# Buffers of their own for q, k and v, and a searched order, in a retention layer with an MLP behind it

## The chip, the cores and the metric

The kernel runs on one core of one Trainium2 chip. The metric is the device time of one execution in microseconds (us), over several runs. The engines are TensorE (PE; its weight loads are listed apart as PEld), VectorE (DVE), ScalarE (ACT), GpSimd (POOL) and SyncE (SP). POOL issues the loads, SP issues the transposing DMAs and the stores.

## The reference

For 8 batches and 8 heads, 576 positions and a head size of 64, retention without softmax: scores times a decay that is zero above the diagonal, times v. Its output is the input of an MLP with an exact Gelu.

```python
scores = scale * np.matmul(q, k.transpose(0, 1, 3, 2))
Dmat = np.where(rel >= 0, gamma[:, None, None] ** rel[None, :, :], 0.0)
attn_out = np.matmul(scores * Dmat[None, :, :, :], v)
x = attn_out.transpose(0, 2, 1, 3).reshape(B * S, H * D)     # 4608 x 512
h = x @ w_in                                                 # 512 -> 2048
g = 0.5 * h * (1.0 + erf(h * inv_sqrt2))
out = g @ w_out                                              # 2048 -> 512
```

## The kernel before

**Units.** The sequence is cut into chunks of 128 positions and a tail of 64. A *unit* is one chunk of one batch, or the tails of a pair of batches: 36 units in all. For each, q and k are turned (head dimension to the partitions), scores are made, masked with the decay, and multiplied with v; a running state (`u_ps`, `u_sb`) carries the earlier chunks. The tile `vh` is v times a decay by head. It is one multiplication on VectorE or, for the units in `VH_ACT` (L174), eight ACTIVATEs, one for each head, on ScalarE (`scaled_v`, L814). Units 0 to 9 are turned by TensorE, the later ones by transposing DMAs that SP issues (`turn_dma`, L603).

**The MLP.** Four units make a block of 512 tokens (`xT`), nine blocks in all. The first layer (`hT`) of blocks 2 to 8 is laid out by `LAYOUTS` (L192): a digit is a *unit of seven products* for a quarter of the hidden features (Strassen's scheme: 28 matmuls of 256 columns, tiles `yT`, `zT`, `xT_`, with sums made by VectorE from `xs` and `wi_sum` and folding on VectorE and ScalarE), and "p" with a digit is a plain quarter (16 matmuls of 512 columns). Two digits in one string are woven together. The second layer (`oT`) uses seven products too, from block 1 on. ScalarE does the Gelus and most copies out of PSUM.

**Loads.** q, k, v and the weights are loaded by POOL in the order of `ORDER` (L196), converted to bf16 on the way; wi and wo are eight blocks of each weight matrix. Units of a pair share a slot. A slot holds q and k in one tile and v in another, from a pool with `N_LD` = 4 buffers (`tiles_of`, L475). A buffer is handed out in turn, and the load waits for the last reader of what was in it.

**The plan.** The kernel's Python code is a list scheduler (`class Plan`, L30): each operation has an engine, an estimated duration, operations it depends on and a due time; the loop at the end takes the operation that can start first. It fixes the order of the instructions on every engine. `Ring` (L263) is what the plan knows of a buffer pool: `take` counts buffers handed out, `give` notes when one comes free, and `at` says when the next may be taken. In before, `at` sorts the times at which buffers come free and takes the n-th. `read` (L494) gives a slot back when q, k and v of both its units have had their last reader. TensorE's choice is in `pe_candidates` (L1543): MLP pieces in their order, and attention stretches (`macros`) when they are due, at least `GAP_A` or `GAP_B` after the stretch before; the groups in `APART` have their scores in a stretch of their own, `BEFORE` us ahead. Up to 16 us, gaps of TensorE are filled with warm-up matmuls (`warm`, L1515).

Of the kernel before, what the change touches and what calls it, by code (L numbers as in the profile page):

```python
# [29 lines left out]
class Plan:  # L30
# [4 lines left out]
    def __init__(self):  # L35
        self.ops = {}
        self.T = dict.fromkeys(self.ENGINES, 0.0)
        self.open = {e: [] for e in self.ENGINES}

# [42 lines left out]

    def start(self, op, engine):
        t = max(self.T[engine], op.ready)
        return max(t, op.at()) if op.at else t
# [13 lines left out]
    def run(self, op, engine, start):  # L99
        op.ran = engine  # L100
        self.T[engine] = self.T["now"] = start + self.dur(op, engine)
        if op.fn:
            op.fn(engine) if op.engine == "any" else op.fn()
        self.done(op, self.T[engine])
# [3 lines left out]
def kernel(  # L108
# [52 lines left out]
    def slot_of(i):  # L161
# [7 lines left out]
    N_LD = 4  # L169
# [4 lines left out]
    VH_ACT = [5, 8, 12, 14, 15, 17, 19, 20, 26, 28, 30, 31, 32, 35, 37]  # L174
# [10 lines left out]
    GAP_A = 4.2  # L185
    GAP_B = 1.5
    APART = [3, 6, 7]
    BEFORE = 0.4
    UNIT_FROM = 2
    LOOK = 16  # L190
    HOLD = 4.6
    LAYOUTS = {2: ['0', '12', 'p3'], 3: ['01', '2', 'p3'], 4: ['2', '30', 'p1'], 5: ['01', '2', 'p3'], 6: ['10', '2', 'p3'], 7: ['01', '23'], 8: ['3', '20', 'p1']}  # L192
    LEAD = 8
    SPREAD = 7.1
    EASE = 6.5
    ORDER = ("q3 q2 k3 q1 pos v2 k2 wi0 k1 wi4 v3 v1 wi1 wi3 wi5 v4 wi2 wi6 k4 wi7 q4 wo0 q5 k5 v5 wo4 wo1 q9 q8 "  # L196
             "wo5 v7 wo6 k7 wo7 v10 wo2 q6 v6 k6 wo3 q7 k10 q10 k8 k9 v9 v8").split()
# [8 lines left out]
    ld_pool = ctx.enter_context(tc.tile_pool(name="ld", bufs=N_LD))  # L206
# [56 lines left out]
    class Ring:  # L263
        def __init__(self, size):
            self.size, self.taken, self.free = size, 0, []

        def at(self):
            n = self.taken - self.size
            return 0.0 if n < 0 else (sorted(w.end + 0.12 if isinstance(w, Landing) else w for w in self.free)[n] if n < len(self.free) else NEVER)

        def take(self):
            self.taken += 1

        def give(self, when):
            self.free.append(when)

    ld_ring, tr_ring, vh_ring, ret_ring, x_ring = Ring(N_LD), Ring(N_QKT), Ring(N_VH), Ring(N_RET), Ring(3)
# [194 lines left out]
    loaded, slots, w_in_sb, w_out_sb = {}, {}, {}, {}  # L472
    touched = {}

    def tiles_of(i):  # L475

        if i not in loaded:
            n = slot_of(i)
            if i in kept:
                loaded[i] = (const.tile([128, 2, H, D], BF16, name=f"qk_ld{i}"), const.tile([128, H, D], BF16, name=f"v_ld{i}"))  # L480
                return loaded[i]
            if n not in slots:
                ld_ring.take()
                slots[n] = (ld_pool.tile([128, 2, H, 2, D], BF16, tag="qk", name="qk_ld"),
                            ld_pool.tile([128, 2, H, D], BF16, tag="v", name="v_ld"))
            qk, v_ld = slots[n]
            j = units[i][2] or 0
            if i in old:
                loaded[i] = (qk.rearrange("p a (j h) b d -> p j a (h b) d", j=2)[:, j], v_ld[:, j])
            else:  # L490
                loaded[i] = (qk[:, :, :, j], v_ld[:, j])
        return loaded[i]

    def read(i, what):  # L494

        n = slot_of(i)
        got = touched.setdefault(n, set())
        got.add((i, what))
        want = {(m, x) for m in pair_with(i) for x in
                ["v"] + (["turn0", "turn1"] if i < N_PE_TR else ["turn"]) + (["state"] if units[i][1] < NCI - 1 else []) + (["inner"] if i in raw else [])}  # L500
        if i not in kept and want <= got:
            ld_ring.give(turning[i] if what == "turn" else T["now"] + 0.12)

    def load_unit(what, i):
        bp, ci, j = units[i]
        qk, v_ld = tiles_of(i)
        src = {"q": q, "k": k, "v": v}[what]
        if j is None:
            both = slots[i][0]
            for jj in range(2):  # L510
                rows = slice(TAIL * jj, TAIL * jj + TAIL)
                dst = v_ld[rows] if what == "v" else both[0:TAIL, "qk".index(what), :, jj]
                nc.gpsimd.dma_start(dst, src[2 * bp + jj, :, ci * C:S, :].rearrange("h s d -> s h d"))
                move(0.68, 0.48)
            return 0.0
        dst = v_ld if what == "v" else qk[:, "qk".index(what)]
        nc.gpsimd.dma_start(dst, src[2 * bp + j, :, ci * C:ci * C + C, :].rearrange("h s d -> s h d"))  # L517
        return move(0.87, LOAD)
# [19 lines left out]
    for item in ORDER:  # L538
        what = item.rstrip("0123456789")
        i = int(item[len(what):] or 0)  # L540
        if what == "pos":
            add("pos", "pool", 0.25, prev, make_pos)
        elif what in ("wi", "wo"):
            add(item, "pool", 0.73, prev, lambda what=what, i=i: load_w(what, i), at=room_to_fly, lag=0.0)
        else:
            def fits(i=i):
                return max(room_to_fly(), 0.0 if i in kept or slot_of(i) in slots else ld_ring.at())
            add(item, "pool", 1.36 if units[i][2] is None else 0.87, prev,
                lambda what=what, i=i: load_unit(what, i), at=fits, lag=0.0)
        prev = [item]  # L550
# [21 lines left out]
    def qkT_of(i):  # L572
        n = slot_of(i)
        if n not in turned_of:
            tr_ring.take()
            turned_of[n] = tr_pool.tile([128, 2, H, TAIL if i in tails else 128], BF16, tag="qkT", name="qkT")
        if i in old:
            return turned_of[n].rearrange("p a (j hp) s -> p j a hp s", j=2)[:, i - n]
        return turned_of[n]
# [3 lines left out]
    def part_of(i, jj):  # L583

        if i in old:
            return loaded[i][0][:, jj], qkT_of(i)[:, jj]
        n = i - slot_of(i)
        return (slots[slot_of(i)][0][:, jj, 4 * n:4 * n + 4].rearrange("p h b d -> p (h b) d"), qkT_of(i)[:, jj, 4 * n:4 * n + 4])
# [14 lines left out]
    def turn_dma(i):  # L603
# [3 lines left out]
        for jj in what:  # L607
            nc.sync.dma_start(qkT_of(i)[:, jj], slots[n][0][rows, jj].rearrange("p h b d -> p (h b d)"), transpose=True)
# [46 lines left out]
    def inner(i):  # L655
        bp, ci, j = units[i]
        s = st[i]
        vals = loaded[i][1] if i in raw else s["vh"]
# [16 lines left out]
    def state(bp, ci):  # L675
# [3 lines left out]
        for h in range(H):  # L679
            for j, i in enumerate(pair_of[bp, ci]):  # L680
                product(u_ps[half(j), h, :], lhsT=loaded[i][0][:, 1, h, :], rhs=st[i]["vh"][:, h, :],
                                 start=(ci == 0 and h == 0), stop=(h == H - 1), skip_group_check=True)
        for i in pair_of[bp, ci]:
            vh_ring.give(T["pe"] + 0.3)
            read(i, "state")
# [44 lines left out]
    def state_atoms(bp, ci, t):  # L730
        return [(N64, [(u_bank[1][half(b), h, :], loaded[i][0][half(t), 1, h, :], st[i]["vh"][half(t), h, :],
# [59 lines left out]
    def gone(nm):  # L791
# [3 lines left out]
        if kind in ("in_b", "in_t"):  # L795
            ret_ring.give(T["pe"] + 0.3)
            tr_ring.give(T["pe"] + 0.3)
            if kind == "in_t":
                vh_ring.give(T["pe"] + 0.3)
        elif kind == "st_b":  # L800
            for i in pair_of[key]:
                vh_ring.give(T["pe"] + 0.3)
# [11 lines left out]
    def scaled_v(i, engine, heads=(0, H)):  # L814
        ci = units[i][1]
        if "vh" not in st[i]:
            vh_ring.take()
            st[i]["vh"] = vh_pool.tile([128, H, D], BF16, tag="vh", name="vh")
        vh = st[i]["vh"]
        if engine == "dve":  # L820
            nc.vector.tensor_tensor(vh, loaded[i][1], dv[:, :, ci:ci + 1].to_broadcast([128, H, D]), op=ALU.mult)  # L821
        else:
            for h in range(*heads):
                nc.scalar.activation(vh[:, h], loaded[i][1][:, h], AF.Copy, scale=dv[:, h, ci:ci + 1])  # L824
# [11 lines left out]
    def evacuate(i, engine):  # L836
# [8 lines left out]
        else:  # L845
            dst = x[:, :, i % 4 * C:i % 4 * C + C]
            b, o = st[slot_of(i)]["o"][j] if i in fine else st[i]["o"]
            if i not in fine:
                out_of_T.add(i)
                if out_of_T >= set(pair_with(i)):  # L850
                    tr_ring.give(T["pe"] + 0.3)
# [15 lines left out]
    tiles_of(0)  # L867
    for nm in "qkv":
        add(f"{nm}0", "any", {"act": 0.6, "dve": 0.83}, [],
            lambda engine, nm=nm: copy_on(engine, loaded[0][1] if nm == "v" else loaded[0][0][:, "qk".index(nm)], first[nm]),  # L870
# [57 lines left out]
    for i in v_order:  # L928
# [4 lines left out]
        if i in VH_ACT:  # L933
# [55 lines left out]
    def g_sum(t, two, which):  # L989
# [9 lines left out]
        nc.vector.tensor_tensor(out_, x0, x1, op=op)  # L999
# [46 lines left out]
    def x_sum(t, which):  # L1046
# [7 lines left out]
        nc.vector.tensor_tensor(xs_tiles[t][:, which], x0, x1, op=op)  # L1054
# [129 lines left out]
    def third(key, width, engine):  # L1184
        m_ring.take()
# [11 lines left out]
    def raw12(key, width, engine):  # L1197
        f_ring.take()
# [4 lines left out]
    def dif(key):  # L1203
        nc.vector.tensor_tensor(chain[key]["q"], chain[key]["X"][1], target(key, "c12") if key[0] == "2" else chain[key]["c12"],
                                op=ALU.subtract)
        if key[0] == "u":
            f_ring.give(T["dve"] + 0.12)
# [10 lines left out]
    def c11(key):  # L1218
# [3 lines left out]
        m_ring.give(T["dve"] + 0.12)  # L1222
# [3 lines left out]
    def first_of(key, width, r):  # L1226
        if "p1" not in chain[key]:
            m_ring.take()
# [7 lines left out]
    def onto(key):  # L1236
        x = chain[key]["B"][1]
        nc.vector.tensor_tensor(x, x, chain[key]["p1"], op=ALU.add)
        m_ring.give(T["dve"] + 0.12)
# [137 lines left out]
    for t in range(FAST, N_BLK):  # L1377
        for two in range(2):
            kps = [2 * two, 2 * two + 1]
            gl = gelus_of(t, kps, 0) + gelus_of(t, kps, 1)  # L1380
            for which in range(4):
                add(f"gs{t},{two}.{which}", "dve", 0.6, gl + ([f"gs{t},{two}.{which - 1}"] if which else []),
                    lambda t=t, two=two, which=which: g_sum(t, two, which),
                    begins["p", t, "5673"[which]] - 1.5 + 0.6 * two,
# [7 lines left out]
    for t in range(N_BLK):  # L1392
        if with_units[t]:
            soon = min(W["u", t, kp, "3"] for kp in with_units[t])
            for which in range(5):
                add(f"xs{t}.{which}", "dve", 0.335, [f"x{i}" for i in range(4 * t, 4 * t + 4)] + ([f"xs{t}.0"] if which else []),
                    lambda t=t, which=which: x_sum(t, which), soon - 3.0 + 0.1 * which, at=xs_ring.at if not which else None)
# [261 lines left out]
```

## Time and profile before

| what | us |
|---|---|
| median of 3 runs | 283.02 (282.54 to 283.83) |
| the profiled execution | 282.72 |
| its span in the profile | 280.7 |
| busy: TensorE, VectorE, ScalarE, POOL | 273.9, 230.1, 174.0, 110.4 |

The span goes from the first to the last instruction of the profiled execution; 2.0 us of its time lie around it. In the page's lists, a group's line is `line engine op out<-in xcount | busy us, mean ns of one | idle before, and what ended it`. A line of the waits is `engine line <- what it waited for: us in total, times, longest us`.

### The profile page before, as it was taken

Reading aid. Unit: us, or ns where it says so; the run is one execution under the profiler, and the core shown is the slowest. Engines: PE = TensorE matmul, PEld = TensorE weight load, DVE = VectorE, ACT = ScalarE, POOL = GpSimd, SP = SyncE. Lnnn points to the kernel's source line nnn. Section 1 sums busy time; section 2 is a strip of 40 time slices with the busy share of each in tenths; the row PEclk is TensorE's granted clock in tenths of the full one; section 3 lists DMA queues with packets and bytes.
Section 4 is the critical chain, followed back from the end, with each engine's and each line's share of the span. In section 5 each row is a group of like instructions: output and inputs, shape, how many; then the busy total and the mean of one; then the engine's idle time right before and its main releaser. Section 6 shows DMA issues by size and latency. Waiting matters only on the chain.

```text
span 280.7 us, 8896 instructions
## 1 busy us (share of the span) xinstructions
PE 273.9 (98%) x3731; PEld 220.0 (78%) x3731; DVE 230.1 (82%) x438; ACT 174.0 (62%) x414; POOL 110.4 (39%) x139
## 2 busy tenths in 40 slices
PE   7999999999999999999999999999999999999993
PEld 2679767578888688868887888688868888888782
DVE  5870465699999998999799999987987799969832
ACT  7678733646438952995297319852898379528740
POOL 8967778847546086233326804705000000000000
PEclk9999999999999999999999999999999999999999
DMA  9999999999999999999989999999800040022013
GB/s 148 165 182 186 178 186 165 142 238 133 127 139 173 197 114 128 140 230 145 156 188 57 134 112 172 210 117 135 184 22 2 6 149 2 4 75 77 0 40 112
DMA packets 152071, 35.57 MB, mean 127 GB/s; under 512 B 141024, under 2 KB 147680, under 8 KB 152032
## 3 DMA queue, kind: packets, MB, share of 16 engines
q0 software_dynamic: 115792, 17.97, 98.1%
q1 hardware_dynamic: 35200, 16.78, 34.9%
q8 instruction: 29, 0.48, 0.8%
q10 hardware_dynamic: 1040, 0.26, 0.4%
q14 instruction: 10, 0.08, 0.1%
HBM read 36.70 MB, written 9.44 MB: 164 GB/s over the span
## 4 chain that ended last, share of the span: by engine, by line
PE 87%; DVE 4%; POOL 4%; DMA 3%; issue 1%; ACT 0%; POOLq 0%; DVEq 0%
PE oT L229 39%; PE hT L229 16%; PE zT L229 10%; PE yT L229 7%; PE o_ps L229 4%; DMA w_in<-in_moe_w_in_dram 3%; PE sc L229 2%; POOL qk_ld L517 2%; PE u_ps L229 2%; DVE s L999 1%; PE qk_ps L233 1%; DVE ret L652 1%; POOL v_ld L517 1%; POOL w_in L523 1%; DVE g L999 0%
## 5 line engine op out<-in xcount | busy, mean ns | idle before, releaser
L229 PEld LDWEIGHTS <-g 128*128 128x128 bf16 x576 | 55.1, 98 | 12.5 <-issue 0.2
L229 PEld LDWEIGHTS <-w_in 128*128 128x128 bf16 x656 | 53.0, 98 | 13.3 <-DMA w_in<-in_moe_w_in_dram 0.4
L229 PE MATMUL hT<-xT,w_in 128*128 128x128 bf16 (+2 forms) x480 | 53.5, 266 | 0.3 <-DMA w_in<-in_moe_w_in_dram 0.3
L229 PEld LDWEIGHTS <-wi_sum 128*128 128x128 bf16 x440 | 42.8, 98 | 6.6
L1099 ACT ACTIVATE g<-hT 128x512 bf16<-128x512 f32 (+1 forms) x72 | 35.9, 505 | 19.5 <-PE hT L229 17.7
L229 PE MATMUL oT<-w_out,g 128*128 128x256 bf16 (+1 forms) x320 | 45.6, 294 | 0.0
L517 POOL DMA_DIRECT2D qk_ld<-in_q_dram x31 | 28.0, 905 | 35.1 <-DMA qkT<-qk_ld 22.8
L229 PEld LDWEIGHTS <-s 128*128 128x128 bf16 x384 | 36.8, 98 | 5.6 <-DVE s L999 0.5
L517 POOL DMA_DIRECT2D v_ld<-in_v_dram x31 | 28.1, 910 | 22.8 <-ACT vh L824 9.5
L229 PE MATMUL oT<-w_sum,s 128*128 128x256 bf16 x256 | 32.4, 273 | 0.2 <-ACT o_sb L1243 0.2
L824 ACT ACTIVATE vh<-v_ld,dv 128x64 bf16<-128x64 bf16 x112 | 31.2, 346 | 1.0 <-DMA v_ld<-in_v_dram 1.0
L229 PE MATMUL oT<-w_sum,g 128*128 128x256 bf16 x256 | 30.8, 273 | 0.0
L517 POOL DMA_DIRECT2D qk_ld<-in_k_dram x31 | 28.0, 903 | 5.5 <-DMA v_ld<-in_v_dram 5.2
L1243 ACT COPY o_sb<-oT 128x512 f32<-128x512 f32 (+1 forms) x27 | 14.5, 538 | 25.2 <-PE oT L229 13.3
L1212 ACT ACTIVATE g<-zT 128x512 bf16<-128x512 f32 x44 | 25.9, 614 | 0.1
L652 DVE TENSOR_TENSOR ret<-sc,msk 128x512 bf16<-128x512 f32 x36 | 23.2, 687 | 1.4 <-PE sc L229 1.4
L1247 DVE TENSOR_TENSOR o_sb<-o_sb,oT 128x512 f32<-128x512 f32 (+1 forms) x27 | 16.8, 629 | 8.8 <-PE oT L229 4.5
L570 ACT COPY q<-yT 128x512 f32<-128x512 f32 x18 | 10.3, 594 | 21.8 <-PE yT L229 21.8
L855 DVE TENSOR_TENSOR xT<-o_ps,dqT 128x512 bf16<-128x512 f32 x26 | 16.8, 686 | 3.3 <-PE o_ps L229 3.3
L821 DVE TENSOR_TENSOR vh<-v_ld,dv 128x512 bf16<-128x512 bf16 x22 | 15.0, 688 | 3.4 <-DMA v_ld<-in_v_dram 3.4
L1221 DVE TENSOR_TENSOR zT<-q,zT 128x512 f32<-128x512 f32 x22 | 15.3, 695 | 1.0 <-PE zT L229 0.6
L1191 DVE TENSOR_TENSOR q<-q,zT 128x512 f32<-128x512 f32 x22 | 14.5, 684 | 1.7 <-PE zT L229 0.8
(170 smaller groups left out, 453.6 us busy)
## 6 DMA issues: line engine op xcount, KB each, us to landing
out_dram<-o_sb SPq DMA_DIRECT2D x30, 256.0 KB, 3.9
qk_ld<-in_q_dram POOLq DMA_DIRECT2D x31, 128.0 KB, 7.6
qk_ld<-in_k_dram POOLq DMA_DIRECT2D x31, 128.0 KB, 8.5
v_ld<-in_v_dram POOLq DMA_DIRECT2D x31, 128.0 KB, 8.0
w_in<-in_moe_w_in_dram POOLq DMA_DIRECT2D x8, 256.0 KB, 8.6
w_out<-in_moe_w_out_dram POOLq DMA_DIRECT2D x8, 256.0 KB, 7.8
out_dram<-o_sb SPq DMA_DIRECT2D x12, 128.0 KB, 2.7
v_ld<-in_v_dram POOLq DMA_DIRECT2D x8, 64.0 KB, 6.4
```

Source lines behind the costliest of these rows:

```text
L229: return nc.tensor.matmul(*args, **more)
L517: nc.gpsimd.dma_start(dst, src[2 * bp + j, :, ci * C:ci * C + C, :].rearrange("h s d -> s h d"))
L652: nc.vector.tensor_tensor(r, t, by, op=ALU.mult)
L821: nc.vector.tensor_tensor(vh, loaded[i][1], dv[:, :, ci:ci + 1].to_broadcast([128, H, D]), op=ALU.mult)
L824: nc.scalar.activation(vh[:, h], loaded[i][1][:, h], AF.Copy, scale=dv[:, h, ci:ci + 1])
L855: nc.vector.tensor_tensor(dst, o, dqT[:, :, ci * C:ci * C + C], op=ALU.mult)
L1099: nc.scalar.activation(g_of(t, m0)[:, m0 % 2:m0 % 2 + n, m0 // 8, lo:hi], hT, AF.Gelu)
L1191: nc.vector.tensor_tensor(q_, q_, chain[key]["Z"][1], op=ALU.subtract)
L1212: nc.scalar.activation(target(key, what), chain[key][n][1], AF.Gelu)
L1221: nc.vector.tensor_tensor(to, chain[key]["q"], z, op=ALU.add)
L1243: nc.scalar.copy(target(key, what), chain[key][n][1])
L1247: nc.vector.tensor_tensor(to, to, chain[key][n][1], op=ALU.add)
```

## The change

The pool of load buffers becomes three: q has three buffers, k five, v four, each with a ring of its own, so that a buffer comes free with the last reader of its own tensor. `Ring` now notes who took which buffer, and `at` waits for the one that is next in turn; the vh and qkT rings are keyed in the same way. Four more units' `vh` stand on ScalarE (18 of the 36 instead of 14). Block 5 has two units of seven products and two plain quarters instead of three and one; other blocks have their parts in another order. The load order and seven of the plan's constants (`GAP_A`, `GAP_B`, `BEFORE`, `HOLD`, `LEAD`, `SPREAD`, `EASE`) are new, and group 5 is added to `APART`. Lists for work on POOL (`VH_POOL`, `XS_POOL`, `GS_POOL`) are there and empty; with them empty, the new `port` in `Plan` delays nothing.

```diff
-    N_LD = 4
+    N_LD = {"q": 3, "k": 5, "v": 4}
...
-    VH_ACT = [5, 8, 12, 14, 15, 17, 19, 20, 26, 28, 30, 31, 32, 35, 37]
+    VH_ACT = [5, 7, 9, 13, 14, 15, 17, 18, 20, 22, 23, 26, 27, 29, 31, 33, 34, 35, 37]
+    VH_POOL = []
+    XS_POOL = []
+    GS_POOL = []
...
-    GAP_A = 4.2
-    GAP_B = 1.5
-    APART = [3, 6, 7]
-    BEFORE = 0.4
+    GAP_A = 0.9
+    GAP_B = 0.5
+    APART = [3, 5, 6, 7]
+    BEFORE = 4.7
...
-    HOLD = 4.6
-    LAYOUTS = {2: ['0', '12', 'p3'], 3: ['01', '2', 'p3'], 4: ['2', '30', 'p1'], 5: ['01', '2', 'p3'], 6: ['10', '2', 'p3'], 7: ['01', '23'], 8: ['3', '20', 'p1']}
-    LEAD = 8
-    SPREAD = 7.1
-    EASE = 6.5
-    ORDER = ("q3 q2 k3 q1 pos v2 k2 wi0 k1 wi4 v3 v1 wi1 wi3 wi5 v4 wi2 wi6 k4 wi7 q4 wo0 q5 k5 v5 wo4 wo1 q9 q8 "
-             "wo5 v7 wo6 k7 wo7 v10 wo2 q6 v6 k6 wo3 q7 k10 q10 k8 k9 v9 v8").split()
+    HOLD = 5.3
+    LAYOUTS = {2: ['0', '12', 'p3'], 3: ['3', '20', 'p1'], 4: ['2', '30', 'p1'], 5: ['3', '2', 'p0', 'p1'], 6: ['2', '3', '0', 'p1'], 7: ['10', '23'], 8: ['2', '30', 'p1']}
+    LEAD = 8.8
+    SPREAD = 7.3
+    EASE = 8.9
+    ORDER = ("q3 k2 pos k1 q2 q1 k3 v2 v1 wi0 wi4 v3 wi5 wi1 wi6 wi2 v4 wi7 wi3 q5 wo0 k4 k5 q4 v5 wo4 k7 wo1 wo5 "
+             "v10 q9 wo2 q6 wo6 q8 wo7 k6 v6 v7 wo3 q7 q10 k10 k9 k8 v8 v9").split()
...
         def at(self):
-            n = self.taken - self.size
-            return 0.0 if n < 0 else (sorted(w.end + 0.12 if isinstance(w, Landing) else w for w in self.free)[n] if n < len(self.free) else NEVER)
+            n = len(self.taken) - self.size
+            w = self.free.get(self.taken[n], NEVER) if n >= 0 else 0.0
+            return w.end + 0.12 if isinstance(w, Landing) else w
...
-    ld_ring, tr_ring, vh_ring, ret_ring, x_ring = Ring(N_LD), Ring(N_QKT), Ring(N_VH), Ring(N_RET), Ring(3)
+    ld_ring = {what: Ring(N_LD[what]) for what in "qkv"}
+    tr_ring, vh_ring, ret_ring, x_ring = Ring(N_QKT), Ring(N_VH), Ring(N_RET), Ring(3)
...
-            if n not in slots:
-                ld_ring.take()
-                slots[n] = (ld_pool.tile([128, 2, H, 2, D], BF16, tag="qk", name="qk_ld"),
-                            ld_pool.tile([128, 2, H, D], BF16, tag="v", name="v_ld"))
+        if (what, n) not in slots:
+            ld_ring[what].take(n)
+            slots[what, n] = ld_pool.tile([128, 2, H, D] if what == "v" else [128, H, 2, D], BF16, tag=what, name=f"{what}_ld", bufs=N_LD[what])
...
-        want = {(m, x) for m in pair_with(i) for x in
-                ["v"] + (["turn0", "turn1"] if i < N_PE_TR else ["turn"]) + (["state"] if units[i][1] < NCI - 1 else []) + (["inner"] if i in raw else [])}
-        if i not in kept and want <= got:
-            ld_ring.give(turning[i] if what == "turn" else T["now"] + 0.12)
+            want = set()
+            for m in pair_with(i):
+                if i < N_PE_TR:
+                    want |= {(m, x) for x in ("turn0", "turn1") if kinds[x] == kind}
+                elif i in tails or kind == "qk"[m - n]:
+                    want |= {(m, "turn")} if kind != "v" else set()
+                want |= {(m, "state")} if kind == "k" and units[i][1] < NCI - 1 else set()
+                want |= {(m, x) for x in ["v"] + (["inner"] if i in raw else [])} if kind == "v" else set()
+            if want <= got:
+                ld_ring[kind].give(turning[i] if what == "turn" else T["now"] + 0.12, n)
...
-            def fits(i=i):
-                return max(room_to_fly(), 0.0 if i in kept or slot_of(i) in slots else ld_ring.at())
+            def fits(what=what, i=i):
+                return max(room_to_fly(), 0.0 if i in kept or (what, slot_of(i)) in slots else ld_ring[what].at())
```

## The prediction

> **What bounds the kernel now.** I read the page's busy times first, then TensorE's waits, then the busy times by stretch, then the timeline at the two places where TensorE does lose time.
>
> ```profile
> span 280.7 us, 8896 instructions
> PE 273.9 (98%) x3731; PEld 220.0 (78%) x3731; DVE 230.1 (82%) x438; ACT 174.0 (62%) x414; POOL 110.4 (39%) x139
> PEclk9999999999999999999999999999999999999999
> ```
>
> ```profile
> PE warm L229 <- DVE ln_scale L347: 1.2, 1, 1.2
> PE hT L229 <- DMA w_in<-in_moe_w_in_dram: 0.3, 1, 0.3
> PE oT L229 <- ACT o_sb L1243: 0.2, 1, 0.2
> ```
>
> These are all of TensorE's waits: it waits once for a load (the third weight block at 19.1 us) and never for q, k or v. Busy time of pipelined matmuls can hide gaps, so I also took the time from each matmul's start to the next one's and compared it with the median for the same pair of shapes. From the 49th hT matmul (19.64) to the last matmul the medians add up to 253.4 us, and the stream took 256.2. So 2.8 us is all that a perfect feeding of TensorE could give back there. Six places hold 1.0 of it: 72.4 (0.12), 82.8 (0.14), 160.3 (0.28), 161.0 (0.14), 192.3 (0.16), 242.4 (0.14). The rest is crumbs below 0.06.
>
> ```profile
> 62.00:90.00 28.00, 28.00 (x384) 24.08 (x383) 28.00 (x59) 15.33 (x34) 17.82 (x22) 1.00 2.09 148
> 146.00:162.00 16.00, 15.79 (x258) 12.22 (x256) 15.74 (x27) 9.46 (x21) 10.91 (x13) 1.00 1.64 95
> ```
>
> Columns: stretch, its length, then busy time (instructions) of PE, PEld, DVE, ACT, POOL. VectorE has no free time in either stretch, and four of the six places lie in them. In the second, TensorE's sequencer waited for a copy that waited for VectorE:
>
> ```profile
> 159.33 0.70 DVE L1238 TENSOR_TENSOR oT<-oT,q 128x512 f32<-128x512 f32 x1 [0.22 <-issue]
> 160.07 0.59 ACT L1243 COPY o_sb<-oT 128x512 f32<-128x512 f32 x1 [2.53 <-DVE oT L1238]
> 160.70 0.60 PE L229 MATMUL oT<-w_sum,s 128*128 128x256 bf16 x4 [0.21 <-ACT o_sb L1243]
> ```
>
> So three things can move the end: the start (up to about 19 us, where TensorE runs warm-up matmuls for want of data), the total of matmul work, and VectorE's two full stretches.
>
> **Part 1: buffers of their own for q, k and v; the plan hands them out in turn.** POOL waits long for free buffers:
>
> ```profile
> POOL qk_ld L517 <- DMA qkT<-qk_ld: 22.8, 3, 9.4
> POOL qk_ld L513 <- PE u_ps L229: 14.7, 2, 10.2
> POOL v_ld L517 <- ACT vh L824: 9.5, 1, 9.5
> ```
>
> All loads queued behind such a wait are late with it, and the transposing DMAs behind them on SP's queue, with the stores behind those. But by the order of the built program a transposed tile is first used 10 to 44 us of matmul time after its transpose is issued, 18 or more from the third pair on, and a transpose takes 8.6 us to land. This cover took in all the lateness of before (TensorE's waits name none). In the changed order the same distances are 10.5 to 40 us, again 18 or more from the third pair on. A q buffer now comes free with its transpose instead of with the last reader of q, k and v. I cost the part at 0. If the cover were gone, the first two pairs (10.5 and 12.3 us against 8.6) would show it first. 133 loads and 30 transposes stay.
>
> **Part 2: the start.** The load order moves wi0 from the seventh load to the ninth and puts k1, q1, k3, v1 ahead of it. Landings of before by the trace: the first at 7.50, then every 0.90; from the twelfth on, 0.85 for a q, k or v block and 1.33 for a weight block (19.99, 21.29; 23.53, 24.85). By the same steps the changed order lands v1 at 13.8, wi0 15.1 (before 12.81), wi4 16.5 (14.94), v3 17.3 (15.84), wi5 18.7. The third weight block of before came 1.2 later than these steps, at 19.14; with that, wi5 comes at 19.9. First-layer pieces of the first block (eight 128x128 matmuls, 11.79 / 26 = 0.453 us each):
>
> ```profile
> 18.30 0.62 PE L229 MATMUL hT<-xT,w_in 128*128 128x128 bf16 x8
> 19.18 11.79 PE L229 MATMUL hT<-xT,w_in 128*128 128x128 bf16 x208 [0.26 <-DMA w_in<-in_moe_w_in_dram]
> ```
>
> Before has done five at 19.18, starts the seventh at 19.63 and is dense from there. In the new order I place the pieces by landing and by the durations of copies (0.59) and masks (0.64): wi0 with unit 1's rows at 15.1; then another after unit 2's value product at 15.9; wi4 twice from 16.5 to 17.4; the state product and unit 3's value product (0.35 each) to 18.1; two pieces to 19.0, or 0.2 less where starts overlap; so the seventh at about 18.9. That is 0.7 earlier, and both streams have the same medians behind that piece. Bounds: 0 if wi5 comes at 19.9 or later and the next blocks with it (the two first blocks' eight pieces are used up at 19.8), 1.3 if no gap at all is left from 16.5 on. I take **-0.7**, since the landing steps are measured and the cast of q0, which now stands behind the position table on VectorE, ends at about 6.0, still before the warm-ups end at 6.3.
>
> **Part 3: matmul work.** 3731 matmuls become 3715: four fewer warm-ups, and block 5 has two fast units and two plain quarters instead of three and one. A unit is 28 matmuls of 256 columns at 109.7 ns = 3.07 us, a plain quarter 16 of 512 at 221.1 = 3.54: +0.47. The new order switches less often between attention and the MLP, though; summed over its whole order with the medians of each pair of shapes, the stream from the 49th hT matmul on is 253.4 us again. **0.0**, with +0.5 as the upper bound.
>
> **Part 4: VectorE and ScalarE.** Four units' vh move to ScalarE, and a unit's folding goes. By the mean of each form VectorE loses 2.7 us of durations in all, ScalarE gains 7.5. What matters is where, in 14 us of matmul time: 62-76 has 18.3 before and 18.2 after, 76-90 16.9 and 16.7, so the places at 72 and 83 stay. 146-160 falls from 16.5 to 15.1, and 230-244 from 16.2 to 15.7. VectorE starts an operation every 0.60 while one lasts 0.69 (the timeline at 146 to 162), so 14 us hold about 16.1 of durations: 146-160 drops below full. Removed: 0.28 + 0.14 at 160, perhaps 0.14 at 242. I take **-0.4** (0 to -1.0, all six places). What is late next is a ScalarE copy, below.
>
> The smaller gaps between attention stretches and the earlier scores of groups held apart move no work; I give their unknown new waits **+0.0**, -0.3 to +0.7.
>
> Sum: 282.72 (the profiled execution: 280.7 span and 2.0 around it) - 0.7 + 0.0 - 0.4 = 281.6. The median of the runs shown is 283.02, 0.3 above that execution, so the forecast for a median is **281.9**.
>
> **The rivals.**
>
> *The start gains nothing.* wi5 at 19.9 and the blocks behind it each come as TensorE asks for them; only part 4 is left: 283.0 - 0.4 = 282.6. For: the 1.2 us delay did occur in before at just this time. Against: each block feeds 4 x 0.453 = 1.8 us and takes 1.33 to land.
>
> *More than forecast.* 1.3 at the start and all six places: 283.0 - 2.3 = 280.7. Against: VectorE stays full from 62 to 90.
>
> *Slower: ScalarE becomes the late engine.* A vh is eight ACTIVATEs on ScalarE:
>
> ```profile
> L824 ACT ACTIVATE vh<-v_ld,dv 128x64 bf16<-128x64 bf16 x112 | 31.2, 346 | 1.0 <-DMA v_ld<-in_v_dram 1.0
> L821 DVE TENSOR_TENSOR vh<-v_ld,dv 128x512 bf16<-128x512 bf16 x22 | 15.0, 688 | 3.4 <-DMA v_ld<-in_v_dram 3.4
> ```
>
> At 32.28 in the timeline eight take 2.02, 0.5 for each part of two. The changed order puts 4 x 4 = 16 more such parts between the gelus and copies that free PSUM banks, above all at 146-160 (ScalarE 10.0 to 14.2 in 14 us) and 216-230 (9.0 to 14.0). If a third of them holds a bank up by its length, that is 16 x 0.5 / 3 = 2.7, and with the start's gain 283.0 + 2.7 - 0.7 = 285.0. It decides once ScalarE's share passes what before bore: 26.0 in the 28 us from 188 to 216, with 0.16 lost. Against: in equal stretches of 28 the new order has at most 26.0.
> The Trainium skill ("ScalarE: Activation LUTs", "Rules for kernel authors") says to multiply on VectorE and not on ScalarE, which speaks against this move. By that rule four units would cost 4 x (2.02 - 0.60) = 5.7 us of engine time; the trace agrees on the price of one, but that it reaches the end needs VectorE to be the freer engine, and here it is not.
>
> *Instructions come late.* The page counts 29 instruction packets, 0.48 MB, 16 KB each, on q8. The densest 128 matmuls of before took 4.5 us (188.2 to 192.7), with a loss of 0.16 at 192.3. The new order has attention bunched near 205, where 128 matmuls take 3.7 by medians: 0.8 tighter, so about +1.0 on top of the forecast, 282.9.
> The Trainium skill ("Runtime: NRT & Kernel Launch", "Instruction fetch mechanics") says that crossing such a 16 KB boundary is mostly hidden; the 0.16 agrees, and no run here shows a tighter one.
>
> **How the numbers follow.** 0.5% is 1.4 us, about what a measurement of this kernel can tell from no change; faster means below 281.6. Forecast 281.9 (281.0 to 282.5): 0.40, of which 0.14 below 281.6. Start gains nothing: 0.18. More than forecast: 0.14. ScalarE late: 0.20. Instructions late: 0.08. Faster 0.14 + 0.14 = 0.28; within 0.5% 0.26 + 0.18 + 0.08 = 0.52; slower 0.20. Low end 280.2: the larger gain and 0.5 more. High end 285.3: the ScalarE case at its price and 0.3 more; beyond lies half of its chance.
>
> **What would show it.** Right: the hT run of the first block dense from before 19 us; no waits at 160; VectorE's busy time about 2.5 lower, ScalarE's about 7 higher; POOL's waits for buffers much shorter and the end hardly moved by that. Wrong: waits of TensorE for w_in at 20 to 27; waits of oT or hT for ScalarE at 146-160 or 216-230; any wait for qkT.

## The result, and the profile after

The changed kernel took 285.04 us (median of 6 runs, 284.52 to 285.75) against 282.70 (282.40 to 283.83) for the kernel before on the same chip: ratio 1.0079, interval 1.0056 to 1.0101. It is slower by 2.3 us; the forecast was 281.9. The profiled execution took 284.71 (span 282.9), against 282.72 (280.7) before. Medians here count every execution, while ratios and their intervals leave out the few slow ones, such as 288.95 and 708.2 among the twelve of experiment 8.

Page of after, its span, busy times and clock:

```profile
span 282.9 us, 8892 instructions
PE 274.5 (97%) x3715; PEld 218.5 (77%) x3715; DVE 227.5 (80%) x434; ACT 178.9 (63%) x440; POOL 110.5 (39%) x139
PEclk9999999999999999999999999999999999999998
```

TensorE's waits in after:

```profile
PE warm L239 <- DVE ln_scale L359: 1.2, 1, 1.2
PE oT L239 <- issue: 0.5, 1, 0.5
PE o_ps L239 <- issue: 0.5, 1, 0.5
PE zT L239 <- ACT g L1237: 0.4, 1, 0.4
PE qk_ps L243 <- DMA k_ld<-in_k_dram: 0.3, 1, 0.3
```

Two of the four new ones wait for "issue", that is, for nothing that the profile shows, and no semaphore is behind them. None waits for qkT.

Starts of matmuls against the medians of before give the account. From the 49th hT matmul to the last one, the work is 253.4 us by medians in both kernels; before lost 2.8 on top of it, after 5.4. With the start, which comes 0.6 earlier, that is the 2.0 us between the two profiled executions. The places of the added loss:

- **30 to 32 us, 0.70**: turns of units 4 and 5 wait for k4, k5 and q4, which the new order issues behind q5 and wo0.
- **147 us, 0.52**: a zT matmul waits for a bank that a gelu has to free, and that gelu stands behind two ACTIVATEs of a vh on ScalarE.
- **188.8 and 195.7 us, 0.65 and 0.64**: the "issue" stops.
- Small ones of 0.07 to 0.1, 0.5 in all. Gone are before's 0.42 at 160/161, 0.13 at 242 and 0.16 at 192. Together this makes 2.3 of the added 2.6; the rest is smaller still.

Timeline of after at these places (start, length, engine, line, operation, count, idle before it and what ended it):

```profile
30.72 0.61 PE L243 MATMUL qk_ps<-ident,k_ld 128*128 128x128 bf16 x8 [0.33 <-DMA k_ld<-in_k_dram]
...
147.06 0.57 ACT L846 ACTIVATE vh<-v_ld,dv 128x64 bf16<-128x64 bf16 x2
147.54 1.07 ACT L1237 ACTIVATE g<-zT 128x512 bf16<-128x512 f32 x2
148.17 0.49 PE L239 MATMUL zT<-xs,wi_sum 128*128 128x256 bf16 x3 [0.36 <-ACT g L1237]
...
188.79 0.19 PE L239 MATMUL o_ps<-ret,vh 64*64 64x64 bf16 x1
189.45 0.19 PE L239 MATMUL o_ps<-ret,vh 64*64 64x64 bf16 x1 [0.46 <-issue]
...
195.17 0.82 PE L239 MATMUL oT<-w_out,s 128*128 128x256 bf16 x6
196.47 0.38 PE L239 MATMUL oT<-w_out,s 128*128 128x256 bf16 x2 [0.47 <-issue]
```

The last two stops lie inside runs of equal matmuls. They are 128 matmuls apart (behind the 2520th and the 2648th), and 29 packets of 16 KB on q8 for 3715 matmuls are one for each 128. I call every such place a *page limit*, and the time from a limit to the start of its packet on q8 its *lag*. (The profile counts two instructions for a matmul, with its weight load, and one for each of some twenty semaphore instructions; the stops of experiment 6 are 1149 matmuls and 7 of these apart, 2305 instructions, so a limit comes every 256 to within one or two.) After the limit at 181.3 the packet came 5.5 us late; DMA queues of after from 181.3 to 186.7, then to 188.2 (packets, MB, and the summed time of the packets as a share of 16 engines, which can pass 100%):

```profile
q0 software_dynamic: 2806, 0.35, 152.0%
q1 hardware_dynamic: 1769, 0.44, 67.0%
...
q0 software_dynamic: 542, 0.07, 214.0%
q1 hardware_dynamic: 292, 0.07, 36.2%
q8 instruction: 1, 0.02, 4.8%
```

There is no q8 line in the first stretch. In the second the packet runs from 186.8 to 188.0, and TensorE goes on at 189.45, 1.5 us after its end. The same limit before had a lag of 3.4, with 5 loads issued and not yet landed; after has 7. From 181 to 189 the loads' queue q0 took more packet time in after than in before; that of transposes and stores, q1, moved more packets but took less. First before, then after:

```profile
q0 software_dynamic: 3782, 0.48, 132.4%
q1 hardware_dynamic: 1615, 0.40, 62.9%
```

```profile
q0 software_dynamic: 3938, 0.49, 161.0%
q1 hardware_dynamic: 2106, 0.52, 53.0%
```

POOL's waits for buffers, the largest of after (before: 22.8, 14.7, 9.5). Its loads wait less and run further ahead: the last one is issued at 183.4, in before at 194.9, and from 175 to 195 us 5.7 loads are in flight on average, in before 3.5.

```profile
POOL v_ld L538 <- ACT vh L846: 15.3, 4, 10.1
POOL k_ld L538 <- DMA qkT<-k_ld: 8.2, 1, 8.2
```

### The profile page after: what moved, and what is told of

The parts are those of the page before. It is cut to its first block, busy times and chain, and to the rows that moved or that the text cites. A ratio compares the mean times of both kernels' runs of the same rounds, so it can differ in the third digit from the quotient of the medians.

```text
span 282.9 us, 8892 instructions
## 1 busy us (share of the span) xinstructions
PE 274.5 (97%) x3715; PEld 218.5 (77%) x3715; DVE 227.5 (80%) x434; ACT 178.9 (63%) x440; POOL 110.5 (39%) x139
## 4 chain that ended last, share of the span: by engine, by line
PE 84%; DMA 6%; POOL 4%; DVE 2%; issue 1%; ACT 1%; POOLq 0%; DVEq 0%; ACTq 0%
PE oT L239 40%; PE hT L239 14%; PE zT L239 9%; PE yT L239 6%; PE o_ps L239 4%; DMA k_ld<-in_k_dram 3%; DMA w_in<-in_moe_w_in_dram 3%; PE sc L239 3%; PE u_ps L239 2%; POOL k_ld L538 1%; PE qk_ps L243 1%; POOL q_ld L538 1%; POOL v_ld L538 1%; POOL w_in L544 1%; DVE q L1216 1%
## 5 line engine op out<-in xcount | busy, mean ns | idle before, releaser
L239 PE MATMUL hT<-xT,w_in 128*128 128x128 bf16 (+2 forms) x496 | 57.3, 269 | 0.0
L1124 ACT ACTIVATE g<-hT 128x512 bf16<-128x512 f32 (+1 forms) x76 | 38.2, 513 | 17.7 <-PE hT L239 15.7
L239 PEld LDWEIGHTS <-wi_sum 128*128 128x128 bf16 x420 | 40.8, 98 | 7.5 <-issue 0.6
L846 ACT ACTIVATE vh<-v_ld,dv 128x64 bf16<-128x64 bf16 x144 | 39.2, 345 | 0.3 <-ACT g L1124 0.3
L538 POOL DMA_DIRECT2D k_ld<-in_k_dram x31 | 27.7, 894 | 19.0 <-DMA qkT<-k_ld 8.2
L538 POOL DMA_DIRECT2D q_ld<-in_q_dram x31 | 27.8, 898 | 12.1 <-DMA k_ld<-in_k_dram 7.3
L1237 ACT ACTIVATE g<-zT 128x512 bf16<-128x512 f32 x42 | 24.4, 613 | 0.5 <-PE o_ps L239 0.4
L239 PE MATMUL oT<-w_out,s 128*128 128x256 bf16 x128 | 15.8, 272 | 0.5 <-issue 0.5
L589 DVE COPY qkT<-qk_ps 128x512 bf16<-128x512 bf16 x15 | 6.0, 421 | 12.5 <-PE qk_ps L243 12.5
L591 ACT COPY q<-yT 128x512 f32<-128x512 f32 x14 | 8.2, 593 | 11.5 <-PE yT L239 11.5
```

What stands on the lines that cost most here:

```text
L239: return nc.tensor.matmul(*args, **more)
L538: nc.gpsimd.dma_start(loaded(what, i), src[2 * bp + j, :, ci * C:ci * C + C, :].rearrange("h s d -> s h d"))
L589: nc.vector.tensor_copy(dst, src)
L591: nc.scalar.copy(dst, src)
L846: nc.scalar.activation(vh[:, h], loaded("v", i)[:, h], AF.Copy, scale=dv[:, h, ci:ci + 1])
L1124: nc.scalar.activation(g_of(t, m0)[:, m0 % 2:m0 % 2 + n, m0 // 8, lo:hi], hT, AF.Gelu)
```

## The experiments

In all of them the plan's order stays as it is, but for the instructions named. Ratios are to the kernel before on the same chip, measured beside it (282.6 to 282.8 us). A stop "at 188.8" is the same place in the program in each variant of after.

**1. Loads of units 4 and 5 earlier.** (The order of issue, not code.)

```diff
-issue order: ... wi3 q5 wo0 k4 k5 q4 v5 ...
+issue order: ... wi3 k4 k5 q5 q4 wo0 v5 ...
```

> The changed kernel with only the order of four loads altered: k4 and k5 are issued ahead of q5, and q4 ahead of the weight block wo0. Theory: the stops of TensorE at 30.16 (0.50 us) and 31.55 (0.20) in the changed kernel are turns of units 4 and 5 that wait for k4, k5 (landed at 29.98, 30.58 there) and q4 (31.68). Moved ahead by one or two loads of 0.85 us, k4 and k5 land at about 29.1 and 30.0, and both stops go: 0.5 to 0.7 us less to the end, about 284.4 against 285.0. Rival: these stops are not the cause but a place where TensorE is paid in any case (wo0 or q5, now 1 to 2 us later, stop it a little behind): the 0.7 shows up again between 30 and 45 and the time stays at 285.0.

Measured: 284.80 us, ratio 1.0079 (1.0054 to 1.0105). Both stops of 30 to 32 are gone, and at the stop of 147 TensorE is 0.43 earlier than in after. The time did not follow: the stop at 188.8 was 1.42 in this profile. So the place is right, but over the variants without a limit on loads that one stop ranges from 0.65 to 1.98, which hides a 0.5 us mend.

**2. The last unit's loads and transposes late.** (`late` is emptied behind matmul 2660, with a dependency on it.)

```diff
-                nc.gpsimd.dma_start(dst, src[...])
+                late.append(start) if i in (N_U - 1,) else start()
...
-            nc.sync.dma_start(qkT_of(i)[:, jj], ..., transpose=True)
+            late.append(start) if i in (N_U - 1,) else start()
```

> The changed kernel with the six loads of the last tail unit (issued from 178.7 to 184.1 there, landed 190.5 to 194.2) and its two transposes held back until matmul 2660 (about 196.4), as late as the kernel before had them. Theory: the stops of 0.65 at 188.79 and 0.64 at 195.72, exactly at the 128-matmul page limits of TensorE's instruction stream with no semaphore to wait for, are instruction packets that came 5.4 to 6.6 and 4.6 to 5.8 us after the limit before, because the loads and transposes were filling the DMA engines at that time. Held back, the packets come at +2 to +4 us, as in the kernel before, and both stops go: 0.6 to 1.3 us less, 283.7 to 284.4 against 285.0. Rival: the stops come from the density of the matmuls there (128 matmuls in 8.1 and 7.0 us) or from other transfers, and both stay, whatever the loads do: 285.0.

Measured: 284.09 us, ratio 1.0045 (1.0027 to 1.0062). The stop at 195.7 is gone (one load in flight at its limit, lag 3.1), that at 188.8 was 1.98: 6 loads issued earlier were still in flight at 181.4, and the lag was 6.1. The time lies in the range that the text gave, but of the two stops it counted on only one went, so that is luck.

**3. Only its transposes late.** (The second half of the edit above.)

> As the run with the last tail unit held back, but only its two transposes are held until matmul 2660; its six loads stay as early as in the changed kernel. It tells transposes from loads. If the loads delay the instruction packets, both stops (0.65 at 188.79, 0.64 at 195.72) stay: 285.0. If the transposes do (SP's at 186.29, 191.20 and 192.50 in the changed kernel lie just ahead of the packets), the one at 195.72 goes, that at 188.79 stays: 284.4.

Measured: 286.42 us, ratio 1.0111 (1.0083 to 1.0140), a stop of 1.97 at 188.8 and none at 195.7. The slower time is in part the clock, told at the end. Since the first stop put the second limit off, a missing second stop proves little in either run.

**4. The vh part behind the gelus.**

```diff
-            for h in range(*heads):
-                nc.scalar.activation(vh[:, h], ...)
+            if parts[0] == 37:
+                behind.append([2, scale_heads])
```

> The changed kernel with one piece of ScalarE's order altered: the two ACTIVATEs of a vh part at 147.06 (0.57 us) go behind the two gelus that stand after them. Theory: TensorE's stop of 0.52 at 147.44 (zT waits for the bank that the gelu has to free) is this vh part, which the changed kernel moved from VectorE to ScalarE; without it ahead, the stop falls to 0.2 or less, 0.3 to 0.5 us less to the end, and its stop does not come back later: about 284.6 against 285.0. Rival: ScalarE is so full there that the vh part only stops TensorE one bank later (within 2 us): the stop moves and the time stays at 285.0.

Measured: 284.66 us, ratio 1.0064 (1.0046 to 1.0081). The stop at 147.4 fell from 0.52 to 0.05, one of 0.14 came at 154.6, and TensorE is 0.3 earlier from there on. Here too the packet stops (1.20 and 1.19) covered it up.

**5. All late transposes held back.** (As 3, with `i in (N_U - 3, N_U - 2, N_U - 1)`.)

> The changed kernel with the last six transposing DMAs of SP (units 33, 34 and the tail unit 35; issued at 183.30, 186.29, 191.20 and 192.50 in the changed kernel, first used at 217.8 or later) held back until matmul 2660 (about 197); all loads stay as they are. It tells transposes from loads, which the two runs before did not: there the stop at 188.8 stayed (1.98 and 1.97 us) while the transposes at 183 to 187 stayed too. If the transposes hold up the instruction packets, the packet of the page limit at 181.5 comes at +2 to +4 us instead of +5.4 to +6.0, both stops (188.8 and 195.7, 1.29 us together in the changed kernel) go, and the time is 283.3 to 284.0 against 285.0. If the loads do, the packet stays at +5.5 or later, the stop at 188.8 stays with 0.6 to 2.0, and the time is 285.0.

Measured: 284.37 us, ratio 1.0067 (1.0055 to 1.0079). The text says six DMAs; it lists the four that were held. The packet came at +6.0, and the stop stayed:

```profile
PE o_ps L241 <- issue: 1.3, 1, 1.3
```

So the four held transposes are not the cause of the stop at 188.8. Two, issued at 178.87 and 180.23, were still in flight at the limit of 181.4, but before has two at that place as well (177.06 and 179.36). At the limit of 188.8 it is otherwise: 7 loads are in flight there in after, in run 3 and in this run, and the lag is 5.3 and 5.0 with three transposes in flight, and 2.7 here with one. Transposes in flight seem to add to the lag; what share of it at 181.3 is theirs was not tried.

**6. The buffers alone, in the old order.**

```diff
-                slots[n] = (ld_pool.tile([128, 2, H, 2, D], BF16, tag="qk", name="qk_ld"),
-                            ld_pool.tile([128, 2, H, D], BF16, tag="v", name="v_ld"))
+                slots[n] = ([ld_pool.tile([128, H, 2, D], BF16, tag=x, name=f"{x}_ld", bufs=BUFS[x]) for x in "qk"],
+                            ld_pool.tile([128, 2, H, D], BF16, tag="v", name="v_ld", bufs=BUFS["v"]))
```

> The kernel before, in its own order, with one thing of the change: buffers of their own for q, k and v (three, five, four) in place of four shared ones; the plan does not know of it, so every engine's program stays, and only POOL's waits for free buffers, and what is queued behind them, become shorter. Prediction on record: it costs nothing and gains nothing, 282.7. Theory now: loads and then transposes come several us earlier; the pair of transposes that started at 189.85 and 191.82 moves to about 183 to 187, ahead of the instruction packets of the page limits at 181 and 188, which then come over 5 us after their limits; stops of TensorE of 0.3 to 1.5 us at 188 or 192 and 0.3 to 1.5 us more to the end, 283.0 to 284.2. Rival of the theory: the stops belong to the new order of matmuls, not to the buffers, and no stop appears.

Measured: 285.83 us (284.80 to 287.94), ratio 1.0131 (1.0100 to 1.0162): 3.2 us slower, more than the whole change, and above the 283.0 to 284.2 of the text. In two of the six executions the mean clock was 0.991 and 0.992, against 0.997 or more in the others, so a part of the median may be the clock, as in run 3; in the profiled one it was 0.997. Every engine's program is that of before. TensorE's waits and its timeline:

```profile
PE oT L230 <- issue: 2.9, 4, 1.5
...
109.04 0.71 PE L230 MATMUL oT<-w_out,s 128*128 128x256 bf16 x5
110.84 0.60 PE L230 MATMUL oT<-w_out,s 128*128 128x256 bf16 x4 [1.10 <-issue]
...
193.32 0.60 PE L230 MATMUL oT<-w_sum,s 128*128 128x256 bf16 x4
195.43 0.50 PE L230 MATMUL oT<-w_sum,s 128*128 128x256 bf16 x3 [1.51 <-issue]
```

Both stops, 1.26 and 1.68 by the medians (before: 0 and 0.16), are at page limits; they make up the 2.84 by which the last matmul starts later (278.65 against 275.81). At the limit before each, 6 loads (one of them just being issued) and 8 were in flight, where before had 3 and 4. The one at 109 no text had looked for. So the buffers alone bring such stops; the new order with the old buffers was not run.

**7. Three mends at once.** (The edits of 1, 4 and 5.)

> The changed kernel with three mends at once: k4, k5 and q4 loaded ahead of q5 and wo0 (took the stops of 0.50 and 0.20 at 30 to 32 away); the vh part of 147 behind the two gelus (took 0.5 away); the last six transposes held until matmul 2660. Theory: the three parts of the loss add up, 0.7 + 0.5 + 1.3, so the span is 2.2 to 2.5 shorter than that of the changed kernel: 282.5 to 282.9, level with the kernel before or just below it, since the gain of 0.6 at the start stays and small stops of some 0.5 remain. If the loads and not the transposes hold up the instruction packets: 0.7 + 0.5 only, 283.8.

Measured: 284.51 us, ratio 1.0059 (1.0034 to 1.0085); above both times of the text; stops at 30 and 147 gone, at 188.8 still 1.75 with 7 loads in flight. The edit of 5 does not mend that stop, as run 5 had shown. At the next limit the lag was 2.9, again with 7 loads and one transpose in flight.

**8. Own buffers, old order, at most three loads in flight.** It takes away what the theory blames and leaves the buffers.

```diff
+    fetched, DEPTH, FROM = [], 3, 40
+    def fetch(dst, src):
+        one = nc.gpsimd.dma_start(dst, src)
+        fetched.append(one.ins.name)
+        if len(fetched) > FROM:
+            tc.add_manual_dep(one.ins, fetched[-1 - DEPTH], ...)
+        return one
```

> The kernel before in its own order with buffers of its own for q, k and v, as in the run that took 285.8 us, and one wait more: from the 41st load of q, k or v on, a load is issued only when the third load before it has landed, so that three at most are in flight instead of up to eight. Theory: what the own buffers cost is only that more loads are in flight at a page limit (6 to 8 at the limits before its two stops, 1.26 us at 109.5 and 1.68 at 193.7) and the instruction packet queues behind them; with three in flight the packets come at +1 to +3 us, both stops go, and the time is back at 282.6 to 283.1. Rival: it is the transposes, or which buffers are read and written, that hold the packets up; then the stops stay and the time is 285 to 286. Third case: three in flight feed too little, and waits for qkT or v appear, 283.5 or more with the stops gone.

> The kernel before with buffers of its own and three loads in flight at most, profiled once more for an undisturbed trace: 283.2 us as in its timed runs, packets at +0.5 to +3 behind their limits, no stop at 109.5 and 193.7.

Measured: 283.22 us, ratio 1.0025 (1.0011 to 1.0040); measured again 283.46, 1.0030 (1.0009 to 1.0050). Both stops are gone, the mean lag from the 7th to the 21st limit falls from 3.0 to 1.3 (trace of the second measurement). That trace shows the third case that the first text named, in another place:

```profile
PE oT L230 <- ACT o_sb L1253: 1.6, 1, 1.6
...
161.76 0.59 ACT L1253 COPY o_sb<-oT 128x512 f32<-128x512 f32 x1 [1.63 <-DMA out_dram<-o_sb]
```

A copy waits for the store that frees its buffer. That the store was queued on SP behind transposes waiting for loads is read from SP's order and was not tried.

**9. Three loads in flight in the changed kernel, alone and with the mends of 1 and 4.**

> The changed kernel with the same wait alone: three loads in flight at most from the 41st load of q, k or v on. Theory: at the limits at 181.3 and 188.8, 7 loads were in flight and the packets came at +5.5 and +5.3; with three they come at +1 to +3, both stops (1.3 to 2.4 us together in the runs so far) go, and the time is 283.0 to 283.8 against 285.0; the stops at 30 to 32 (0.7) and 147 (0.5) stay. Rival: the loads in flight are not what delays the packets (holding the last unit's six loads back, or all late transposes, left the stop at 188.8 in place), and the time is 285.0.

> The changed kernel with the three mends that each took a stop away: k4, k5 and q4 loaded ahead of q5 and wo0 (0.7), the vh part of 147 behind the two gelus (0.5), three loads in flight at most (1.3 or more). Theory: the loss is made of these three and they add up: 285.0 - 2.5 = 282.5 or down to 281.9, no slower than the kernel before and perhaps 0.5 faster by what remains of the start. Rival: mended stops come back as others behind them, 283.5 or more.

Measured: 283.46 us, ratio 1.0030 (1.0018 to 1.0042), and 283.22, 1.0026 (1.0014 to 1.0038). In the first, neither packet stop is left (lags 2.5 and 3.4), and the stops at 31.5 and 147 stay. The second missed its 281.9 to 282.5: in its profiled execution (283.50) the start's gain is missing, the 49th hT matmul coming at 19.87, and small stops of 0.15 and 0.17 are left at 154.7 and 188.6.

**10. Five in flight.** (`DEPTH` 5: the old order with own buffers; the changed kernel alone; the changed kernel with the mends of 1 and 4.)

> As the run of the kernel before with buffers of its own and three loads in flight at most (283.2 us; without that limit 285.8), but with five in flight. By the profiles so far the packet of a page limit comes 1.6 us after it with one to three loads in flight (mean over 60 limits), 3.0 with four or five (5 limits), 4.0 with six to eight (83 limits), and a stop has been seen only where it came 3.2 or later. Theory: the lag grows with the depth, so the packets come at about +3 at the limits near 102 and 189, one of the two stops or a part of them is back, 0 to 1.3 us, and the time lies between: 283.2 to 284.8. Rival: only the full queue of eight does harm, or the gain of pacing came from something else than the depth (transposes later, other buffers); then it is 283.2 or less, with the lag as with three.

> The changed kernel with nothing but five loads in flight at most. Theory: both packet stops go, those at 30 to 32 (0.2 to 0.7) and 147 (0.5) stay: 283.2 to 283.8 against 285.0, as with three in flight (283.46). Rival: with five in flight the lag at the limits at 181.3 and 188.8 is still over 3.5 and one stop stays: 284 to 284.5.

> The changed kernel with the three mends at once, as before with three in flight (283.2), but with five loads in flight at most: k4, k5 and q4 ahead of q5 and wo0, the vh part of 147 behind the two gelus, five in flight. Theory: with five, the packets still come in time (b3: mean lag 2 us, no stop) and no store is held up by late loads, so the three parts of the loss go (0.7, 0.5, 1.3 or more) and nothing new comes: 282.2 to 282.8, level with the kernel before (282.7) or up to 0.5 below it by what is left of the start. Rival: the new order has a loss of its own beyond the three (crumbs, the start given back), and it stays at 283.2.

Measured: old order 283.04 us, ratio 1.0011 (1.0001 to 1.0021); changed kernel 283.36, 1.0025 (1.0011 to 1.0038); with both mends 282.84, 1.0011 (1.0002 to 1.0020). Five in flight let the packets through, and TensorE waits for no store. The first of the three texts expected a part of the stops back, 283.2 to 284.8; none came, and the mean lag over the 7th to the 21st limit is 1.7. This run also parts loads from transposes. At the limit before the stop of 109, the old order with own buffers had 5 or 6 loads and two transposes in flight and a lag of 5.3; with five at most, 3 loads, again two transposes, and 3.0. Before the other stop it was 8 loads, one transpose and 3.2; with five at most 2 loads, two transposes and 0.6. The stops went with the loads, not with the transposes. In the changed kernel with five in flight the lags at 181.3 and 188.7 are 4.0 and 2.6; the first is over the 3.5 at which the text expected a stop, but there was time enough to the next limit. TensorE's waits of the changed kernel with five in flight and nothing else:

```profile
PE warm L239 <- DVE ln_scale L359: 1.2, 1, 1.2
PE zT L239 <- ACT g L1246: 0.4, 1, 0.4
PE oT L239 <- issue: 0.2, 1, 0.2
```

Of the 0.79% that the change cost, five in flight gives back 0.54 (1.5 us) and the two mends 0.14 (0.4 us). The 0.11% left, 0.3 us, was not traced to a place. No version was faster than the kernel before.

## Why the prediction was wrong

**Part 1, buffers, "I cost the part at 0": the step that failed.** Its working was right for what it looked at: no matmul waited for qkT in any kernel. But it asked only who reads the loaded data. Loads that stop waiting for buffers also leave more transfers in flight, and the instruction packets then come later. Worth in after: 1.29 us in the profiled execution, 1.5 by the run with five in flight; in the old order 3.2 in the medians.

**Rival "Instructions come late": right victim, wrong cause, wrong place.** It took the time between two limits as the quantity that changes, and put the danger near 205; the page that takes least time in after goes from 209.7 to 213.5, 3.8 us. Nothing was lost there: with no load in flight the lag is 1.1. (Its 4.5 us for the densest 128 matmuls of before is not the least: the 128 from 209.4 on take 2.9, with no stop.) A stop comes when the lag, the packet's 1.2 and the 1.5 after it exceed the time to the next limit: 181.3 + 5.5 + 1.2 + 1.5 = 189.5 against 188.8. Worked out with each packet's own time for the 420 steps from limit to limit in 15 profiles, this sum names all eleven stops above 0.3 us that lie at a limit; elsewhere it never asks for more than 0.41, and that at before's 0.16 at 192. At 0.08 it had too small a chance; the page gave the 29 packets, and their lags in before (up to 5.2) could have been read from the trace.
The Trainium skill ("Runtime: NRT & Kernel Launch", "Instruction fetch mechanics") calls the crossing of such a boundary mostly hidden. The prediction let that stand beside its 0.16; most limits agree, but two of 29 cost 1.29 us in after and 2.94 in the old order with own buffers.

**Part 2, the start, -0.7: right at its place, gone 12 us later.** The 49th hT matmul starts at 19.04 against 19.64. In means over the seven profiles of the changed start order without the first mend it is 19.14 (19.00 to 19.41), over four of the old 19.79 (19.64 to 19.93): -0.65. But by the 256th hT matmul -0.25 of these means is left (31.55 against 31.80), and in after against before -0.1 (31.55 against 31.65). In after k4, k5 and q4 take it; in others also a wait for w_in at 20 us, one of the signs named as "wrong". In the sum the +0.7 of 30 to 32 belongs to the term for unknown new waits, whose upper end was +0.7 for the whole run.

**Part 3, matmul work, 0.0: right as far as medians can tell.** Both streams are 253.4 us by the medians used there; with pairs of shapes grouped in other ways the difference between the two kernels goes from -0.3 to +0.8.

**Part 4, VectorE, -0.4: right, though ScalarE's stop at 147 takes as much back.** The stops at 160, 161 and 242 (0.55) are gone, VectorE's busy time fell by 2.6 (2.7 was said), ScalarE's rose by 4.9 (about 7 was said). The stretches of before, in after (length; PE, PEld, DVE, ACT, POOL):

```profile
62.00:90.00 28.00, 27.95 (x389) 23.95 (x384) 28.00 (x58) 15.72 (x37) 15.97 (x21) 1.00 2.00 156
146.00:162.00 16.00, 15.64 (x256) 11.95 (x255) 14.46 (x24) 12.88 (x35) 5.94 (x8) 1.00 1.09 90
```

From 146 to 162 VectorE is no longer full, and ScalarE has gone from 9.46 to 12.88; from 62 to 90 VectorE stays full; the stop at 72 is what it was, that at 83 has grown from 0.14 to 0.21.

**Rival "ScalarE becomes late" (285.0, 0.20): its time came out, its mechanism only for a fifth.** One bank of the five or so that it assumed was held up, at 147, as it said: 0.52 of the 2.3 us. That the time agrees is luck.

## What to carry to other kernels

Ask of a freed buffer or an earlier transfer not only who waits for its data, but what else has to come by DMA beside it: here the instruction stream itself, with a stop that no semaphore shows ("issue", at steps of about 128 matmuls). More buffers want a limit on the transfers in flight; five here took back most of what own buffers cost, while three held up a store in one profile. When single stops vary by 1 us from profile to profile, judge a 0.5 us mend by its place in the trace, and by time only once the large stops are gone.

## What the runs showed of the hardware

**The lag of an instruction packet grows with the loads in flight.** Over the 7th to the 23rd limit of 15 profiles, with loads counted that POOL has issued and that have not landed:

| loads in flight | limits | mean lag, us | from, to |
|---|---|---|---|
| 0 | 51 | 0.4 | -2.6, 1.9 |
| 1 to 3 | 101 | 1.6 | -0.9, 4.4 |
| 4 or 5 | 20 | 2.8 | 1.8, 5.2 |
| 6 to 8 | 83 | 4.0 | 2.5, 6.7 |

The Trainium skill ("DMA: Bandwidth & Descriptors", "Queues, rings and completion order") says that a DMA engine takes turns between its queues, packet by packet. By that alone the depth of one queue should not matter; here it does. Where the packet waits is not shown. The number of loads is not all of it either: of the limits with 6 to 8 loads in flight, those with no transpose in flight had a mean lag of 2.8 (5 limits), with one 3.0 (11), with two 4.1 (49), with three 4.3 (16). Nor are full DMA engines: in run 5 they moved 37 GB/s from 182.6 to 183.6, against 160 in the 1.3 us before, and the packet of the limit at 181.4 still came at 187.3.

**TensorE resumed 1.2 to 1.6 us after the end of the late packet** in ten of eleven stops (2.4 in the other).

**The clock was halved once, right after a stop.** In run 3 the granted clock was 0.5 (of full speed) from 191.07 to 194.49, for 3.41 us, soon after the stop of 1.97 (188.76 to 190.73). All its stretches are multiples of 3.413 us (180.906 = 53 times, 88.747 = 26 times), as are those of before and after (269.653 = 79 times, then 0.5 behind the last matmul). The stop lay within one such window (187.66 to 191.07). One of 1.98 that fell across two windows in run 2 did not do it, nor did one of 1.78 inside a window (193.13 to 196.54) in run 6; so one case shows it, and what it takes stays open. The Trainium skill ("TensorE: Matmul & The Clock Gate", "Part 1: The HAM clock gate") gives a free-running window of 3413 ns, and the lengths agree.
